# An RWKV-7 recurrence with a feed-forward interleaved: transposes of y, a decay, third blocks and feed-forward pieces change places

## The chip, the cores and the metric

The kernel runs on one core of one Trainium2 chip. The metric is device time in microseconds, the median of several runs. A core has five engines with an instruction queue each: TensorE (PE; the loading of weights is shown apart as PEld), VectorE (DVE), ScalarE (ACT), GpSimd (POOL) and SyncE (SP), which here does nothing but issue DMAs. An engine takes its instructions in program order, so an instruction that waits holds up all that stand behind it on that engine.

## The reference

Two stages. The first is a recurrence over 768 time steps for 4 batches of 8 heads with head size 40; the second sends its output, as 3072 tokens of 320 features, through a feed-forward with 2048 hidden units.

```python
for t in range(S):
    y[:, :, t] = np.einsum('bhd,bhde->bhe', rt, state)
    Sa = np.einsum('bhde,bhe->bhd', state, at)
    state_decay = state * wt[:, :, None, :] - np.einsum('bhd,bhe->bhde', Sa, bt)
    state = state_decay + np.einsum('bhd,bhe->bhde', vt, kt)
...
h = x @ w_in                        # x: (3072, 320)
g = h * np.clip(h + 3.0, 0.0, 6.0) / 6.0
out = g @ w_out
```

## The kernel before

The recurrence is computed in chunks of 64 time steps. A **unit** is one chunk of two of the four batches, all heads: 128 tokens. There are 24 units, numbered 0 to 23; even units hold the state of one pair of batches, odd units that of the other. Within a chunk the steps are solved with a triangular inverse per head, which is made for four units at once: `invert` is a chain of over sixty small DVE operations (L822 and L828), and two **third blocks** per four units (`third_block`, for the first and the last two units) complete the inverse with matmuls in two halves: L858, copies by ACT (L866), then L882, copies by ACT (L892).

The work of a unit is cut into named stages, and a stage into its PE matmuls and what DVE, ACT or POOL make of their result. Ahead of a unit's own turn come W and gam (decay products), A, B, K, factor, F, KB, E and EV. In its turn come RT and VT (transposes of r and v), S (the state transposed, L970), R, C, U, UT, rS, H, and `ysn` (L1099), which gives y and the state's update at once. DVE adds y's parts (L1106) and POOL scales the result into the tile `yg` (L1107). `scale` multiplies the state by the unit's decay: POOL makes the factor (L932, L933), DVE multiplies (L934).

`move` and `move2` bring `yg` into the layout that the feed-forward reads: eight DMAs from `yg` to `xt` on SP's queue (L1147 and L1152), four each. SP also issues all loads of inputs (L470 and L473; the loads for V, B and K of later units are recorded in stages C and KB, in slot 3) and the writes of the output (L1268). They go in the order in which they are recorded.

The feed-forward is a generator that gives a **piece** of PE work at each call. A unit has two jobs; a job has four pieces that expand (`expand`, L1203, each matmul shown as two records, so eight records a piece) and four that contract (`contract`, L1244, four records a piece). Eight short matmuls over the last 64 features (the narrow part) are put in by themselves, mostly at the head of a slot. ACT and DVE (L1218, L1219) form the activation between expansion and contraction, and a job's contraction follows the expansion of the next job. Expansion of a unit can be recorded only when its `move2` has been recorded; on the chip its first matmul waits until the first four DMAs have landed.

The order of all this is written out by hand. Units 0 to 3 have an order of their own. Units 4 to 7 go through `earlier_blocks`: four blocks a unit, each with two halves (`together`), and behind each half as many pieces as `rate / 2` has added up to. From unit 8 on, `slot(i, j)` records the five slots of unit `i` by the list `SLOTS`, where `(5, "W")` is a stage of the unit five later and `(-1, "ysn")` one of the unit before. So y of unit `i - 1` is made in slot 3 of unit `i`. Behind each slot stands a gap:

```python
    def gap(rate, between=None):
        pieces_due[0] += rate
        n = int(pieces_due[0])
        pieces_due[0] -= n
        for k in range(n):
            if between and k == n // 2:
                between()
            piece()
```

`rate` is 3.6 (`DENSE`) while an inversion runs, else 2.7 (`NORMAL`), and 2.2 in units 8 and 9. `between` records half of a third block: for the first two units of each four, in the gaps behind slots 2 and 3. After the last slot, the pieces that are left follow in a row: the tail.

PSUM is taken in pairs of banks; from unit 8 on there are two pairs in turn, which attention stages and third blocks share.

Of the kernel before, what the change touches and what calls it, by code (L numbers as in the profile page):

```python
# [31 lines left out]
def kernel(  # L32
# [47 lines left out]
    NU = 2 * NP  # L80
# [193 lines left out]
    for i, (x, y) in enumerate([(0, DFF // 2), (0, NJ // 2)]):  # L274
        for n, z in enumerate((x, y)):
# [4 lines left out]
            name = ("WA", "BK")[i][n]  # L280
# [164 lines left out]
    NK = NG * NU  # L445
# [101 lines left out]
    def begun_beside():  # L547

        for n, name in enumerate("KB"):
            x = area[:, SCAN + 1 + n * H * JOIN:SCAN + 1 + (n + 1) * H * JOIN]  # L550
            nc.gpsimd.memset(x, 0.0)
            beside[name] = x.rearrange("p (h t) -> p h t", h=H)

    def begun_fixed():

        beside["S"] = grp.tile([P, 2, 2, P], F32, name="S", tag="S", bufs=1)
        nc.gpsimd.memset(beside["S"][:], 0.0)
        beside["E"] = grp.tile([P, H, BL], F32, name="E", tag="U", bufs=1)
        nc.gpsimd.memset(beside["E"][:], 0.0)
# [338 lines left out]
    def third_blocks(first=False):  # L898

        zs = inv.tile([P, 2, 2, H, L], F32, name="zs", tag="x", bufs=1)  # L900
        return [third_block(*third[-1], 2 * n, zs[:, n], first) for n in range(2)]
# [373 lines left out]
    side = deque()  # L1275
    owed, due = [0.0], [0.0]

    def pieces(n):

        owed[0] += n * (8 / 9 if spread[0] else 1)  # L1280
        while owed[0] >= 1:
            owed[0] -= 1
            place[0] = next(stream)
            if not place[0]:
                owed[0] = 0.0

    def aside(n, weight=0):

        for _ in range(n):
            if side and next(side[0], side) is side:  # L1290
                side.popleft()
            due[0] += weight
            while due[0] >= 1:
                due[0] -= 1
                next(weights, None)

    def deal(n):

        for _ in range(n):
            next(weights, None)  # L1300

    def run(stage, steps=0, mixed=0, deals=0):

        for at in stage:
            if at == DONE:
                return
            aside(steps, mixed)
            deal(deals)
# [60 lines left out]
    blocks = {}  # L1369
# [6 lines left out]
    n, cleared = 0, []  # L1376
# [19 lines left out]
    def block(i, j):  # L1396

        if i % NU < 2:
            if j == 0:
                if i % NU == 0:  # L1400
                    blocks[i], blocks[i + 1] = third_blocks()
            run(blocks[i])
# [110 lines left out]
    coming, ahead, own = deque(range(2 * NU, NK)), {}, {}  # L1513

    def a_block(m):

        if coming and begins[coming[0]] == m:
            u = coming.popleft()
            close = coming and begins[coming[0]] < m + BLOCKS
            ahead[u, m] = prepared(u), CLOSE_STAGES if close else AHEAD_STAGES  # L1520
        if m % BLOCKS == 0 and m // BLOCKS + NU < NK:
            i = m // BLOCKS + NU
            own[i, m] = step(i), OWN_STAGES
        parts = {}, {}
        for (u, begin), (fs, order) in sorted(own.items()) + sorted(ahead.items()):
            if m - begin < len(order):
                for name in order[m - begin]:
                    parts[begin % BLOCKS > 0].setdefault(name, []).append(fs[name])
        for k, part in enumerate(parts):
            together(part)  # L1530
            if any(u % NU == NU - 1 and m - begin == 2 and k == (begin % BLOCKS > 0)
                   for u, begin in ahead):
                third.clear()
                side.append(invert(group_F[-1], third))
            yield

    def feed(n, inversion):

        whole = int(n)
        for k in range(whole):  # L1540
            pieces(1)
            aside(inversion)
        pieces(n - whole)

    def earlier_blocks():

        m = 0
        for i in range(NU, 2 * NU):
            spread[0] = i >= 2 * NU - 1
            for j in range(BLOCKS):  # L1550
                rate, inversion = 3.5, 0
                if i < 2 * NU - 1:
                    rate = 2.8
                parts = a_block(m)
                next(parts)
                if side or i % NU == NU - 1:
                    rate, inversion = 6.2, 2 + (i < 2 * NU)
                feed(rate / 2, inversion)
                for _ in parts:
                    pass  # L1560
                if i % NU < 2 and j < 2:
                    if i % NU == 0:
                        aside(3 * L)
                    block(i, j)
                if side:
                    rate, inversion = 6.2, 2 + (i < 2 * NU)
                feed(rate / 2, inversion)
                m += 1

    earlier_blocks()  # L1570


# [4 lines left out]
        [(4, "EV"), (0, "R"), (-1, "H")],  # L1577
        [(5, "A B K factor")],
        [(-1, "ysn"), (0, "C"), (5, "F KB")],
        [(-1, "move move2"), (0, "U UT"), (5, "E"), (0, "rS"), (1, "scale")],  # L1580
    ]
    FIRST_SLOTS = [
        SLOTS[0],
# [8 lines left out]
    NORMAL, DENSE, STEPS_OF = 2.7, 3.6, 2.2  # L1592
    TURNS_NEXT, LEFT = (1, 4), {"e1": 5, "e2": 4, "e3": 3, "e4": 2, True: 1}
    steps_due, pieces_due = [0.0], [0.0]
    units, comings = {u: fs for (u, _), (fs, _) in own.items()}, {u: fs for (u, _), (fs, _) in ahead.items()}

    def piece():

        place[0] = next(stream)
        if side:  # L1600
            steps_due[0] += STEPS_OF
            aside(int(steps_due[0]))
            steps_due[0] -= int(steps_due[0])
        return place[0] is not None

    def gap(rate, between=None):

        pieces_due[0] += rate
        n = int(pieces_due[0])
        pieces_due[0] -= n  # L1610
        for k in range(n):
            if between and k == n // 2:
                between()
            piece()

    def slot(i, j):

        afresh()
        begun, taken = [], {}
        if narrow and (j not in TURNS_NEXT or LEFT[place[0]] < pieces_due[0] + NORMAL):  # L1620
            narrow[0]()
        for k, names_ in (FIRST_SLOTS if i == 2 * NU else SLOTS)[j]:
            u = i + k
            if u >= NK:
                continue
            for name in names_.split():
                if k == 5 and u < 2 * NU + AHEAD:
                    continue
                if name == "W":
                    comings[u] = prepared(u)  # L1630
                if name == "scale":
                    units[u] = step(u)
                rest = (comings if k > 0 and name != "scale" else units)[u][name]()
                fill = [n for n, x in enumerate(FILLS) if name in x]
                if fill:
                    shared[:] = taken.setdefault(fill[0], [None, 0])
                    next(rest)
                    taken[fill[0]][:] = shared
                begun.append((name, rest))
                if name == "F" and u % NU == NU - 1:  # L1640
                    begun.append(("invert", iter(())))
        begun.sort(key=lambda x: AFTER.index(x[0]) if x[0] in AFTER else len(AFTER))
        for _, rest in begun:
            for _ in rest:
                pass
        afresh()
        if begun and begun[-1][0] == "invert":
            third.clear()
            side.append(invert(group_F[(i + 5) // NU], third))

    begun_homes()
    begun_fixed()
    units[2 * NU] = step(2 * NU)
    for _ in units[2 * NU]["scale"]():
        pass
    pairs.clear()
    pairs.append(("pair", 2))
    for i in range(2 * NU, NK + 1):
        for j in range(5):
            if i % NU == 0 and j == 2 and i < NK:  # L1660
                aside(3 * L)
                blocks[i], blocks[i + 1] = third_blocks()
            slot(i, j)
            if i == 2 * NU and j == 1:
                begun_beside()
            gap(DENSE if side else NORMAL if i > 2 * NU + 1 else 2.2,
                (lambda: run(blocks[i])) if i < NK and i % NU < 2 and j in (2, 3) else None)
    spread[0] = False
    while jobs or next(stream):
        next(stream)  # L1670
# [30 lines left out]
```

## Time and profile before

| | |
|---|---|
| median of 3 runs | 820.15 us (818.6 to 824.12) |
| profiled execution | 817.8 us |
| its span, first to last instruction | 816.1 us |
| mean granted TensorE clock | 0.958 |
| DVE, ACT, POOL busy | 487.4, 318.2, 172.3 us |
| feed-forward matmuls, L1203 and L1244 | 254.9 and 230.8 us of PE busy time |
| small DVE steps of the inversion, L822 and L828 | 128.0 us in 360 instructions |

A line of the groups names line, engine, operation, output and inputs, shapes and count; behind the bar stand the busy time, the mean length of one in ns, the idle time of the engine just before and what ended it. In a list of waits a line says who waited for whom, the total in us, how often, and the longest. In a table of windows a line has the stretch and its length, then the busy time and the number of instructions of PE, PEld, DVE, ACT and POOL, the granted clock, the share of the DMA engines and GB/s. In a timeline a line has start, length, engine, line and operation, and in square brackets the idle time before it and what ended it. "issue" stands where the engine waited for nothing that the profile shows.

### The profile page before, as it was taken

The page shows a single profiled execution, that of the slowest core. Times are in us where ns is not written, and L with a number is a line of the kernel's source. Part 1 is how long each engine was busy: PE and PEld are TensorE (multiplying, and loading weights), DVE is VectorE, ACT ScalarE, POOL GpSimd, SP SyncE. Part 2 cuts the span into 40 slices and gives each one's busy share as a digit, 9 for nine tenths or more (in the row PEclk, how much of TensorE's full clock was granted, in tenths as well). Part 3 has the DMA queues.
Part 4 walks back from the last instruction along what each step waited for, and adds up shares of the span by engine and source line. Part 5 has one row for each costly group of instructions (what it writes and reads, how often), then busy time and mean ns, then how long its engine had stood idle before and what let it go on. Part 6 is the DMA issues. An engine that isn't in the chain of part 4 may idle for free.

```text
span 816.1 us, 33536 instructions
## 1 busy us (share of the span) xinstructions
PE 728.8 (89%) x14960; PEld 614.8 (75%) x14960; DVE 487.4 (60%) x967; ACT 318.2 (39%) x646; POOL 172.3 (21%) x322
## 2 busy tenths in 40 slices
PE   5626769999999998999998889998999999999998
PEld 4626658878778787777776778886888888888886
DVE  8897887699545797334886335797436783232210
ACT  2348982313444333542243443334453234321121
POOL 6403003322222304211221221321213021110000
PEclk9855889999999999999999999999999999999999
DMA  9683553311232303221221213222231111100000
GB/s 121 113 194 101 141 135 72 71 28 32 53 70 51 66 19 55 53 45 35 56 48 35 44 33 63 53 45 45 48 56 25 31 27 26 25 19 20 19 9 17
DMA packets 174208, 44.92 MB, mean 55 GB/s; under 512 B 157424, under 2 KB 172784, under 8 KB 174064
## 3 DMA queue, kind: packets, MB, share of 16 engines
q1 hardware_dynamic: 169760, 42.03, 26.2%
q8 instruction: 118, 1.93, 1.0%
q10 hardware_dynamic: 4304, 0.74, 0.6%
q14 instruction: 26, 0.21, 0.1%
HBM read 34.08 MB, written 3.93 MB: 47 GB/s over the span
## 4 chain that ended last, share of the span: by engine, by line
PE 62%; DVE 16%; issue 7%; SPq 5%; ACT 4%; DMA 3%; POOL 1%; ACTq 0%; POOLq 0%; DVEq 0%
PE h L1203 23%; PE o L1244 11%; PE one L1244 7%; DVE prod L822 4%; DVE x L828 4%; PE pair L539 3%; PE pair L1099 3%; SPq L473 3%; PE pair L499 2%; DVE gt L1219 2%; SPq L470 1%; DVE area L565 1%; PE pair L771 1%; PE pair L947 1%; PE pair L997 1%
## 5 line engine op out<-in xcount | busy, mean ns | idle before, releaser
L1203 PE MATMUL h<-xt,win 128*128 128x128 f32 (+1 forms) x2304 | 254.9, 286 | 10.4 <-DMA xt<-yg 7.4
L1203 PEld LDWEIGHTS h<-xt,win 128*128 128x128 f32 (+1 forms) x2304 | 234.2, 195 | 28.3 <-issue 10.5
L1244 PE MATMUL o<-wout,gt 128*128 128x320 f32 x480 | 145.7, 444 | 0.0
L1219 DVE SCALAR_TENSOR_TENSOR gt<-gt,h 128x512 f32<-128x512 f32 x96 | 63.3, 684 | 137.8 <-ACT gt L1218 137.8
L1218 ACT ACTIVATE gt<-h,three 128x512 f32<-128x512 f32 x96 | 62.9, 685 | 167.1 <-PE h L1203 166.9
L1244 PEld LDWEIGHTS o<-wout,gt 128*128 128x128 f32 x480 | 85.9, 190 | 30.9
L1244 PE MATMUL one<-wout,gt 128*128 128x320 f32 x288 | 85.1, 442 | 0.0
L822 DVE TENSOR_TENSOR prod<-x 128x30 f32<-128x30 f32 (+9 forms) x180 | 64.8, 360 | 8.4 <-POOL x L807 3.4
L1244 PEld LDWEIGHTS one<-wout,gt 128*128 128x128 f32 x288 | 52.3, 190 | 19.4
L828 DVE TENSOR_TENSOR x<-x,prod 128x30 f32<-128x30 f32 (+9 forms) x180 | 63.2, 351 | 5.5
L565 DVE COPY_PREDICATED area<-mask,pair 128x512 f32<-128x512 int32 x60 | 44.5, 746 | 32.3 <-PE pair L539 14.7
L1107 POOL TENSOR_TENSOR yg<-ys,gam 128x512 f32<-128x512 f32 x14 | 17.8, 1271 | 191.6 <-DVE ys L1106 144.3
L604 DVE TENSOR_TENSOR_SCAN prods<-area,start 128x528 f32<-128x528 f32 x24 | 30.1, 1259 | 27.1 <-ACT area L584 17.0
L776 ACT ACTIVATE EV<-pair 64x320 f32<-64x320 f32 x44 | 19.0, 431 | 50.9 <-PE pair L947 30.8
L636 POOL COPY gam<-prods 128x256 f32<-128x256 f32 x22 | 12.4, 563 | 108.4 <-DVE prods L604 108.3
L743 POOL TENSOR_TENSOR KBt<-K,rgt 128x320 f32<-128x320 f32 x22 | 19.1, 869 | 60.5 <-ACT rgt L722 58.8
L615 DVE TENSOR_TENSOR_SCAN area<-area,start 128x528 f32<-128x528 f32 x24 | 31.2, 1300 | 0.8
L1106 DVE TENSOR_TENSOR ys<-pair,ys 128x512 f32<-128x512 f32 x16 | 11.1, 691 | 27.9 <-PE pair L1099 27.9
L1099 PEld LDWEIGHTS pair<-area,KBt 64*64 64x64 f32 x1024 | 23.6, 133 | 5.4 <-issue 4.1
L1099 PE MATMUL pair<-area,KBt 64*64 64x104 f32 x1024 | 27.2, 252 | 0.3
L694 ACT ACTIVATE F<-pair 32x256 f32<-32x256 f32 x32 | 11.9, 373 | 34.1 <-PE pair L687 33.9
L637 POOL COPY rgam<-prods 128x256 f32<-128x256 f32 x22 | 24.5, 1114 | 0.0
(300 smaller groups left out, 1101.2 us busy)
## 6 DMA issues: line engine op xcount, KB each, us to landing
V<-in_v_dram SPq DMA_DIRECT2D x96, 40.0 KB
out_dram<-ob SPq DMA_DIRECT2D x47, 80.0 KB
R<-in_r_dram SPq DMA_DIRECT2D x92, 40.0 KB
B<-in_b_dram SPq DMA_DIRECT2D x42, 80.0 KB
K<-in_k_dram SPq DMA_DIRECT2D x42, 80.0 KB
W<-in_w_dram SPq DMA_DIRECT2D x37, 80.0 KB
A<-in_a_dram SPq DMA_DIRECT2D x37, 80.0 KB
xt<-yg SPq DMA_DIRECT2D x72, 40.0 KB
```

Of the source, the lines that this page charges most:

```text
L473: engine.dma_start(out=t[rows, :, 0:D], in_=y.rearrange("h t e -> t h e"))
L565: nc.vector.copy_predicated(out=x[:].rearrange("p (i h) t -> p i h t", i=2), mask=mask8, data=o[2])
L604: nc.vector.tensor_tensor_scan(out=prods[:].rearrange("p r m i -> p (r m i)"), data0=wm[:, 0:SCAN], data1=start[:], initial=0.0, op0=ALU.m ...
L615: nc.vector.tensor_tensor_scan(out=back, data0=back, data1=start[:], initial=0.0, op0=ALU.mult, op1=ALU.add)
L637: nc.gpsimd.tensor_copy(rv[:, :, 0:HB], o["prods"][:, :, 0, 0:HB][:, :, ::-1])
L822: nc.vector.tensor_tensor(out=pv, in0=_ap(x[:], (i + 1) * L + i, [[L, n], [0, i]]), in1=_ap(x[:], i * L, [[0, n], [1, i]]), op=ALU.mult,)
L828: nc.vector.tensor_tensor(out=rest, in0=rest, in1=pv, op=ALU.add)
L1099: nc.tensor.matmul(out=o2[q][half(s), pr, :], lhsT=o[name][half(q), h * D:h * D + SLOT], rhs=beside[name][half(q), 4 * rs + 2 * (s ^ (q * ...
L1203: nc.tensor.matmul(out=hp[c][:, i, :], lhsT=lhsT, rhs=rhs, start=(begun[c] == 0), stop=(begun[c] == 3 * NQ - 1))
L1218: nc.scalar.activation(out=gt[:], in_=hp[c][:], func=AF.Relu, bias=three[:], scale=1.0)
L1219: nc.vector.scalar_tensor_tensor(out=gt[:], in0=gt[:], scalar=6.0, in1=hp[c][:], op0=ALU.min, op1=ALU.mult)
L1244: nc.tensor.matmul(out=op[:], lhsT=gts[c][:, n, :], rhs=wout[:, c * HJ + r * NQ + n, :], start=((split or r == 0) and c == 0 and n == 0), ...
```

## The change

Four things move; no instruction is added or taken away, and the arithmetic is the same.

- In `earlier_blocks` the rate of the blocks of units 4 to 6 is 2.2 instead of 2.8 pieces, so that feed-forward pieces come later. The rate of the gaps of units 8 and 9 is 2.1 instead of 2.2.
- The decay of unit 8, which stood between the last block and the first slot behind two memsets, is recorded behind the third block of unit 7.
- `move` and `move2` of unit `i - 1` are recorded behind the second piece of the gap after slot 3 of unit `i`, not in slot 4. (For unit 7 they stay in slot 2 of unit 8.)
- Third blocks go into other gaps. The first one's halves come behind the third piece after slot 2 and the first piece after slot 3 of the first unit of four; the second one's behind the first piece after slots 0 and 1 of the third unit of four, instead of slots 2 and 3 of the second. These four gaps have the rate 3.6.

```diff
@@ earlier_blocks
                 if i < 2 * NU - 1:
-                    rate = 2.8
+                    rate = 2.2
...
+                if i == 2 * NU - 1 and j == 2:
+                    begun_units[2 * NU] = step(2 * NU)
+                    for _ in begun_units[2 * NU]["scale"]():
+                        pass
@@ SLOTS
-        [(-1, "move move2"), (0, "U UT"), (5, "E"), (0, "rS"), (1, "scale")],
+        [(0, "U UT"), (5, "E"), (0, "rS"), (1, "scale")],
@@
+    THIRDS = {(0, 2): 3, (0, 3): 1, (2, 0): 1, (2, 1): 1}
+
+    def moves(u):
+        for name in ("move", "move2"):
+            for _ in units[u][name]():
+                pass
+
-    def gap(rate, between=None):
+    def gap(rate, between):
...
-            if between and k == n // 2:
-                between()
+            if k in between:
+                between.pop(k)()
             piece()
+        for k in sorted(between):
+            between[k]()
@@ behind begun_fixed()
-    units[2 * NU] = step(2 * NU)
-    for _ in units[2 * NU]["scale"]():
-        pass
@@ the loop over slots
-            gap(DENSE if side else NORMAL if i > 2 * NU + 1 else 2.2,
-                (lambda: run(blocks[i])) if i < NK and i % NU < 2 and j in (2, 3) else None)
+            turn_now = i < NK and (i % NU, j) in THIRDS
+            rate = DENSE if side or turn_now else NORMAL if i > 2 * NU + 1 else 2.1
+            between = {}
+            if j == 3 and 2 * NU < i:
+                between[2] = lambda: moves(i - 1)
+            if turn_now:
+                between[THIRDS[i % NU, j]] = lambda: run(blocks[i - i % NU + i % NU // 2])
+            gap(rate, between)
```

More of the change, by code (lines that the diff above doesn't have):

```diff
@@ L1543, in feed @@
         pieces(n - whole)
+    begun_units = {}
     def earlier_blocks():
@@ L1594 @@
     steps_due, pieces_due = [0.0], [0.0]
-    units, comings = {u: fs for (u, _), (fs, _) in own.items()}, {u: fs for (u, _), (fs, _) in ahead.items()}
+    units, comings = {**begun_units, **{u: fs for (u, _), (fs, _) in own.items()}}, {u: fs for (u, _), (fs, _) in ahead.items()}
     def piece():
```

## The prediction

> **What bounds the kernel.** I read the page's busy rows first, then the stage table, then PE's waits in it.
>
> ```profile
> span 816.1 us, 33536 instructions
> PE 728.8 (89%) x14960; PEld 614.8 (75%) x14960; DVE 487.4 (60%) x967; ACT 318.2 (39%) x646; POOL 172.3 (21%) x322
> ```
>
> PE is busy for 89%. The windows are the blocks of units 4 to 6, of unit 7, the slots of unit 8, units 9 to 24, and the tail:
>
> ```profile
> 195.30:271.00 75.70, 72.56 (x1894) 60.05 (x1893) 41.20 (x74) 37.59 (x88) 19.83 (x36) 1.00 0.32 58
> 271.00:310.40 39.40, 36.39 (x680) 30.72 (x679) 36.65 (x87) 11.63 (x25) 9.50 (x17) 1.00 0.20 37
> 310.40:338.90 28.50, 24.36 (x601) 20.61 (x600) 12.35 (x20) 13.74 (x28) 10.94 (x18) 0.94 0.30 56
> 338.90:772.00 433.10, 412.68 (x8482) 347.65 (x8482) 235.12 (x467) 155.26 (x322) 81.10 (x140) 0.99 0.20 39
> 772.00:816.10 44.10, 40.22 (x266) 32.61 (x264) 5.14 (x8) 6.37 (x11) 0.00 (x0) 1.00 0.06 15
> ```
>
> Length and PE's time are the first two numbers: PE idles 3.1, 3.0, 4.1 and 20.4 us in the four stages before the tail. Work that moves between places where PE is full costs the same in both. So I price the idle, from PE's waits between 195 and 772 us:
>
> ```profile
> PE h L1203 <- DMA xt<-yg: 7.4, 3, 3.6
> PE pair L1055 <- issue: 4.7, 4, 1.6
> PE pair L858 <- DVE bt L660: 4.4, 4, 1.4
> PE pair L970 <- DVE state L934: 2.8, 1, 2.8
> PE pair L882 <- issue: 1.9, 3, 0.8
> PE h L1203 <- DVE start L613: 1.5, 1, 1.5
> ```
>
> Feed-forward waits for its transposed input (L1203), third blocks for a PSUM pair (L858), the ninth unit's S for its decay (L970); L1055 and L882 stand still in the middle of a run for nothing that is shown. A standstill can cost more than its length:
>
> ```profile
> 315.11 0.44 PE L970 MATMUL pair<-ident,state 40*128 40x40 f32 x8 [2.84 <-DVE state L934]
> 315.48 3.67 PE L1203 MATMUL h<-xt,win 128*128 128x128 f32 x16
> ```
>
> and, as windows, the stretch behind it and behind two waits of L1203:
>
> ```profile
> 315.10:319.07 3.97, 3.96 (x24) 3.80 (x24) 2.57 (x3) 1.79 (x4) 1.32 (x2) 0.57 0.33 63
> 369.95:373.00 3.05, 3.05 (x52) 2.83 (x56) 1.55 (x4) 0.00 (x0) 1.47 (x2) 0.52 0.11 30
> 555.00:558.50 3.50, 3.50 (x113) 3.31 (x113) 3.17 (x13) 0.35 (x1) 1.05 (x2) 1.00 0.14 30
> ```
>
> After 2.84 us the granted clock is 0.57 (third number from the right) and sixteen matmuls take 3.67 us, where the chain of waits has 1.98 for sixteen: about 1.6 us more. After 1.89 us (at 369.95) it is 0.52, after 1.85 us (554.99) still 1.00. So I add 1.6 us to a standstill of 1.9 us or more.
>
> **Part 1, feed-forward later.** A piece is 0.99 us of PE if it expands (1.98 for two) and 1.17 if it contracts (2.35 for two). The accumulators give 28 pieces in the blocks of units 4 to 6 instead of 34, 263 instead of 248 in the slots and nine less in the tail. Six pieces, 6.5 us, leave the blocks and return in the slots, nine go from the tail to the slots: zero as long as PE is full. The cover is thinner in the blocks: 1.2 pieces behind each half block instead of 1.4. Ten half blocks have a single piece behind them already, and only one of the halves that follow begins late (0.5 us). I take **+1.5**. Bounds: -3.1 (all idle of this stage goes) and +6.5 (the blocks get no shorter).
>
> **Part 2, the decay.** POOL's scale (0.20 us) and copy and DVE's multiply (0.49 us) go from behind the inversion's copies and two memsets on POOL (311.1 to 314.3) into unit 7's third block. There POOL has been idle for 27 us before 308.3, the state that is scaled was last written at 264.6, and no other unit touches it. DVE gets 0.5 us more while it is busy for 36.65 of 39.40 us, and that delays the transposes at its end, which the third block at 325.7 needs late. Gone: 2.84 us and 1.6 us of half clock, 4.4. Next late is slot 1: ACT evicts RT and VT only until 314.5 us and S behind them, so its products wait for a pair, about 1 us. I take **-3.5**; bounds -4.4 and 0.
>
> [...]
>
> **Part 3, the moves.** In program order they now stand two pieces behind slot 3's products instead of at slot 4. But they are DMAs on SP's queue, behind V, B and K, which slot 3 issues:
>
> ```profile
> 420.24 3.52 SPq L470 DMA_DIRECT2D V<-in_v_dram  x4
> 423.87 1.29 SPq L473 DMA_DIRECT2D B<-in_b_dram  x2
> 425.25 1.28 SPq L473 DMA_DIRECT2D K<-in_k_dram  x2
> 426.58 3.13 SPq L1147 DMA_DIRECT2D xt<-yg  x4
> ```
>
> yg was ready at 418.1, the moves went at 426.6, and PE was released 1.3 us after the fourth. The change passes no more than one output write (1.2 us of SP). So the data come 17 to 18 us after slot 3 begins, as before, and cost or gain is decided by when PE gets there. From unit 14's slots, which have no waits: attention 1.1, 1.6, 1.1, 2.5 and 2.0 us in slots 0 to 4, the narrow matmuls 0.9, half a third block 0.8. For unit 10 of the kernel before: slot 3, 0.9 + 2.5 + three expansions 2.97 = 6.4; slot 4, 2.0 + three contractions and a fourth that ends it 4.7 = 6.7; slot 0, 1.1: 14.2 us, against 17.85 until the data are there, so 3.65 late; the trace has 3.62. With the pieces of the changed kernel:
> - unit 10: 17.4 against 19.1 (an output write now goes first): 1.7 late
> - unit 11: 16.0 against 17.5: 1.5 late
> - unit 12: 18.7 against 18.5: not late
> - unit 13: 17.4 against 18.0: 0.6 late
> - unit 14: 15.2, and 1.1 that its slot 3 lost to DVE, against 18.0: 1.7 late
> - unit 15: 13.9 against 17.3: 3.4 late
> - unit 16: 14.9 against 16.5: 1.6 late
>
> The seven sum to 10.5. Units 8 and 9 have two more gaps and come after their data; from unit 17 on SP has no inputs left to fetch and the data come in time. A mid-run standstill that stays in unit 11's way makes it 9.5, and unit 15 costs 1.6 of clock: 11.1. Before: 1.89 + 1.52 + 3.62 + 1.85 = 8.9 (the wait put down to L613 ends 1.36 after the moves, so it is one of them), and two clock drops: 12.1. I take **-1.0**. Bounds: -12.1 (nothing is late), +18 (all six 2 us later and slowed).
>
> **Part 4, third blocks.** First halves at slot 2 waited 1.37, 1.15, 1.15 and 0.73 us (the 4.4 of L858). The first block now goes behind three pieces, over 3 us, so slot 2's evictions are done; but it then stands right before slot 3, whose second pair waits for its four ACT copies (1.5 us), beside ysn's 1.6: about 0.3 four times. The second block goes behind one piece after slot 0, where RT and VT are evicted 1.9 us after the slot begins and PE arrives after 2.1 to 2.3. 0.1 each where a relu (0.69) stands first. Sum **-2.8**; bounds -4.4 and +4.4 (L858's wait at all eight places).
>
> **Part 5, mid-run standstills.** 4.7 + 1.9 = 6.6 us in seven places, all in slots 3 and 4 behind a third block and gaps of two or three pieces. Units 9 and 13 lose their block there (0.60 + 0.85 + 0.76 = 2.2 us). At the other four gaps have up to one piece more; half of 4.4. **-4.4**; bounds -6.6 and +2 (they come up behind slot 0).
>
> [...]
>
> **Sum:** 1.5 - 3.5 - 1.0 - 2.8 - 4.4 = -10.2. The profiled execution took 817.8 us (its span is 816.1), so 807.6; the median of the runs is 820.15, so **810.0**.
>
> **Rivals.**
> - *Late data (slower).* The second place in this sum that can turn: if units 10, 11 and 13 to 16 reach their data 2 us earlier than worked out (PE fuller of pieces, SP kept up), they idle 10.5 + 12 = 22.5 us and five drop the clock, 8: 30.5 instead of 12.1. Then +18.4 for -1.0: **829**. For it: the kernel before ran into just this four times, and nine pieces more bring feed-forward nearer to its data. Against: the working gives 3.65 for 3.62.
> - *Waits come back.* DVE or ACT, not PE, sets slots 8 to 16, and each wait that goes appears one slot on; the decay and the thinner blocks alone remain, -2: **818**. For it: DVE is 93% busy in unit 7. Against: 54% in units 9 to 24.
> - *The moves do land earlier*, by the two to three pieces that they stand earlier: the lateness goes, -10 more: **800**. Against: SP's order above.
>
> **Chances.** Forecast 0.55 (own range 803 to 816), late data 0.13, waits come back 0.22, earlier moves 0.10. The range 799 to 821 leaves out the slower rival and little else. 1% is 8.2 us, about what a measurement of this kernel can tell from none: under 812 lies most of the forecast and the earlier moves, 0.53; 0.34 within; 0.13 slower.
>
> **What would show it.** L970's wait gone and the clock 1.00 near 315 us; the blocks up to unit 7 ending some 5 us sooner; a tail of about 34 us; waits of L1203 for xt near units 14 to 16 in place of those at 370, 400 and 431 us; L858 near zero; the four issues of xt still right behind V, B and K. I am wrong if xt waits exceed 15 us, or if units 4 to 6 stay at 75 us.

## The result

| | before | after |
|---|---|---|
| median | 819.69 us (20 runs) | 814.96 us (20 runs) |
| ratio | | 0.994, interval 0.9917 to 0.9963 |
| profiled execution, span | 817.8, 816.1 us | 815.24, 813.6 us |
| stretches at half clock between 195 us and TensorE's last matmul | 3 x 3.41 us | 4 x 3.41 us |

The changed kernel is 0.6% faster, 4.7 us. Forecast were 10.2 us: the sign is right and the size about half. The interval lies wholly below 1, but the gain is smaller than 1%, which the prediction took for about the least that a measurement of this kernel can show. The head of the page of the changed kernel:

```profile
span 813.6 us, 33528 instructions
PE 728.0 (89%) x14960; PEld 614.5 (76%) x14960; DVE 487.8 (60%) x967; ACT 318.1 (39%) x646; POOL 170.9 (21%) x322
```

The same five stages of the changed kernel as windows (length, then busy time and number of instructions of PE, PEld, DVE, ACT, POOL; then granted clock, DMA share, GB/s):

```profile
196.60:270.60 74.00, 66.80 (x1858) 55.17 (x1857) 40.49 (x72) 36.40 (x86) 19.95 (x36) 1.00 0.31 57
270.60:308.80 38.20, 35.27 (x667) 29.53 (x665) 35.12 (x88) 11.39 (x25) 8.45 (x19) 1.00 0.24 44
308.80:336.20 27.40, 25.24 (x618) 20.71 (x618) 14.37 (x21) 14.62 (x30) 10.97 (x17) 1.00 0.30 57
336.20:779.70 443.50, 428.49 (x8587) 362.48 (x8587) 236.44 (x469) 157.32 (x325) 81.48 (x140) 0.98 0.19 38
779.70:813.60 33.90, 29.98 (x192) 23.84 (x190) 3.85 (x6) 4.67 (x8) 0.00 (x0) 0.97 0.07 19
```

Length minus PE's time is what PE idles: 7.2, 2.9, 2.2, 15.0 and 3.9 us, where before had 3.1, 3.0, 4.1, 20.4 and 3.9. From the first window to the end 620.8 us became 617.0, that is 3.8 less: 3.4 of idle and 0.4 of PE's busy time. (The stretch ahead of the first window was 1.3 us longer. Its length differs by up to 4.5 us between executions of kernels that are the same there, so I compare from the first window on.) PE's waits in the changed kernel between 195 and 772 us (total, times, longest):

```profile
PE h L1203 <- DMA xt<-yg: 8.3, 3, 3.9
PE h L1203 <- DVE area L615: 2.7, 1, 2.7
PE pair L858 <- ACT EV L776: 2.3, 1, 2.3
PE pair L947 <- DVE area L565: 2.1, 1, 2.1
PE pair L771 <- ACT VT L958: 1.4, 1, 1.4
PE pair L687 <- ACT ys L1061: 1.2, 1, 1.2
PE pair L687 <- issue: 1.0, 2, 0.7
PE pair L1099 <- DVE bt L660: 0.9, 2, 0.7
...
PE pair L499 <- DVE ys L1132: 0.8, 1, 0.8
...
PE pair L1055 <- issue: 0.7, 1, 0.7
```

L970's wait is gone, so are L858's four and nearly all standstills of L1055 and L882. What grew is the wait for xt: the line put down to L615 ends 1.2 us after the fourth DMA of its unit and is one of them, so they sum to 11.4 us with one of 0.4 that stands further down, against 8.9. One such place, on SyncE and on TensorE: the wait for unit 15's y, which PE reaches in the first slot of unit 17.

```profile
568.63 3.12 SPq L470 DMA_DIRECT2D V<-in_v_dram  x4
571.86 1.97 SPq L473 DMA_DIRECT2D B<-in_b_dram  x2
573.92 1.28 SPq L473 DMA_DIRECT2D K<-in_k_dram  x2
575.26 3.12 SPq L1147 DMA_DIRECT2D xt<-yg  x4
```

```profile
575.38 0.39 PE L970 MATMUL pair<-ident,state 40*128 40x40 f32 x8
579.67 5.51 PE L1203 MATMUL h<-xt,win 128*128 128x128 f32 x38 [3.90 <-DMA xt<-yg]
```

yg was complete at 566.7 us. The DMAs that transpose it went 8.5 us later, behind the loads, and PE stood for 3.90 us.

### The profile page after: what moved, and what is told of

The parts are those of the page before. It is cut to its first block, busy times and chain, and to the rows that moved or that the text cites. A ratio compares the mean times of both kernels' runs of the same rounds, so it can differ in the third digit from the quotient of the medians.

```text
span 813.6 us, 33528 instructions
## 1 busy us (share of the span) xinstructions
PE 728.0 (89%) x14960; PEld 614.5 (76%) x14960; DVE 487.8 (60%) x967; ACT 318.1 (39%) x646; POOL 170.9 (21%) x322
## 3 DMA queue, kind: packets, MB, share of 16 engines
q8 instruction: 118, 1.93, 1.0%
## 4 chain that ended last, share of the span: by engine, by line
PE 62%; DVE 21%; ACT 5%; issue 4%; SPq 3%; DMA 2%; POOL 1%; DVEq 0%; ACTq 0%
PE h L1203 22%; PE o L1244 10%; PE one L1244 8%; DVE prod L822 4%; DVE x L828 4%; PE pair L539 3%; PE pair L1099 3%; DVE area L615 2%; DVE prods L604 2%; PE pair L499 2%; DVE gt L1219 2%; SPq L473 1%; PE pair L1039 1%; PE pair L1055 1%; PE pair L997 1%
## 5 line engine op out<-in xcount | busy, mean ns | idle before, releaser
L1203 PE MATMUL h<-xt,win 128*128 128x128 f32 (+1 forms) x2304 | 256.5, 287 | 13.0 <-DMA xt<-yg 8.3
L1203 PEld LDWEIGHTS h<-xt,win 128*128 128x128 f32 (+1 forms) x2304 | 235.9, 195 | 31.5 <-issue 14.2
L1244 PE MATMUL o<-wout,gt 128*128 128x320 f32 x480 | 146.0, 444 | 0.0
L1244 PEld LDWEIGHTS o<-wout,gt 128*128 128x128 f32 x480 | 85.7, 190 | 31.3 <-issue 0.4
L1244 PE MATMUL one<-wout,gt 128*128 128x320 f32 x288 | 85.3, 441 | 0.3 <-issue 0.3
L1244 PEld LDWEIGHTS one<-wout,gt 128*128 128x128 f32 x288 | 52.1, 190 | 19.4 <-issue 0.4
L615 DVE TENSOR_TENSOR_SCAN area<-area,start 128x528 f32<-128x528 f32 x24 | 31.0, 1290 | 0.8
L1099 PEld LDWEIGHTS pair<-area,KBt 64*64 64x64 f32 x1024 | 23.4, 132 | 5.5 <-issue 3.9
L1099 PE MATMUL pair<-area,KBt 64*64 64x104 f32 x1024 | 26.6, 251 | 1.0 <-DVE bt L660 0.9
L722 ACT ACTIVATE rgt<-pair 128x320 f32<-128x320 f32 x16 | 7.0, 438 | 41.4 <-DVE kt L757 37.1
```

What stands on the lines that cost most here:

```text
L615: nc.vector.tensor_tensor_scan(out=back, data0=back, data1=start[:], initial=0.0, op0=ALU.mult, op1=ALU.add)
L1099: nc.tensor.matmul(out=o2[q][half(s), pr, :], lhsT=o[name][half(q), h * D:h * D + SLOT], rhs=beside[name][half(q), 4 * rs + 2 * (s ^ (q * ...
L1203: nc.tensor.matmul(out=hp[c][:, i, :], lhsT=lhsT, rhs=rhs, start=(begun[c] == 0), stop=(begun[c] == 3 * NQ - 1))
L1244: nc.tensor.matmul(out=op[:], lhsT=gts[c][:, n, :], rhs=wout[:, c * HJ + r * NQ + n, :], start=((split or r == 0) and c == 0 and n == 0), ...
```

## The experiments

Each run is compared with the kernel before, run on the same chip. All compute the whole result. Stage lengths are those of the profiled executions.

### Each part alone

**The decay alone**: before, with the decay of unit 8 in unit 7.

```diff
+                if i == 2 * NU - 1 and j == 2:
+                    begun_units[2 * NU] = step(2 * NU)
...
-    units[2 * NU] = step(2 * NU)
```

> The kernel before with only unit 8's decay moved. Theory A (the sum of the prediction, part 2): the wait of L970 (2.84 us) and the half clock behind it (1.6 us) go, about 1 us comes back in slot 1 as waits for pairs; the waits for xt in units 8 to 14 stay as they are, since they hang on the distance from slot 3 to the expansion alone. 816 us against 819.7 (-3.5). Rival B: PE is only earlier at the next wait (xt of unit 8 at 370 us), which grows by what the decay saved: 819 to 820.

Measured: 822.25 against 823.58 us, 0.9986 (0.9956 to 1.0015). Unit 8 takes 24.0 us instead of 28.5, L970's wait is gone, and units 9 to 16 take 244.5 instead of 242.1. Its waits of PE between 195 and 772 us:

```profile
PE h L1203 <- DMA xt<-yg: 5.3, 3, 3.3
PE pair L858 <- DVE bt L660: 4.4, 4, 1.4
PE pair L1055 <- issue: 3.9, 3, 1.9
PE h L1203 <- DVE prod L822: 3.3, 1, 3.3
...
PE h L1203 <- DVE start L613: 1.8, 1, 1.8
```

The three lines of L1203 are waits for xt and sum to 10.4 us, 1.5 more than before, so more than half of the 2.4 us that units 9 to 16 lose is lateness. The saving is real where it is made, and part of it is lost again; the interval holds both none of it and 3.6 us.

**The later feed-forward alone**: before, with the rate of the early blocks at 2.2.

```diff
-                    rate = 2.8
+                    rate = 2.2
```

> The kernel before with only the rate of the blocks of units 4 to 6 at 2.2 instead of 2.8, so every later piece comes some seven pieces later. Theory A (data arrival decides): by the slot costs of the prediction the expansions of units 8 to 16 begin 23 to 34 us behind slot 3, the data need 17 to 19, so all four waits for xt (8.9 us) and the three drops of the clock behind them go, -12 us; the blocks of units 4 to 6 get only about 1.7 us shorter for 6.5 us fewer pieces (as in the trace of the changed kernel), +5: 812 to 813. Rival B (moving pieces is free, the gain of the change is in its other three parts): 819 to 821, or slower by the thinner cover alone, 825.

Measured: 807.3 us, 0.9823 (0.9791 to 0.9854). This single number brings three times what the whole change brings. Its stages and its waits between 195 and 772 us:

```profile
196.10:270.20 74.10, 66.63 (x1859) 54.99 (x1857) 40.47 (x72) 36.45 (x86) 20.11 (x36) 1.00 0.32 57
...
339.70:753.50 413.80, 407.28 (x8473) 344.49 (x8473) 232.46 (x465) 154.92 (x320) 81.63 (x140) 1.00 0.21 40
753.50:805.00 51.50, 47.66 (x314) 38.50 (x313) 6.43 (x10) 7.64 (x13) 0.00 (x0) 1.00 0.06 15
```

```profile
PE pair L858 <- DVE bt L660: 4.5, 4, 1.4
PE pair L970 <- DVE state L934: 3.8, 1, 3.8
PE pair L858 <- ACT EV L776: 2.3, 1, 2.3
```

No wait of L1203 for xt is left. The data of units 8 to 16 are first expanded 22 to 34 us after the products that give y (`ysn`, in slot 3), when they have long landed, because six pieces more are still to be done ahead of them; in the kernel before, the units that waited came to theirs after 17 to 19 us, the wait included. Units 9 to 24 take 413.8 us instead of 433.1, although the thin early blocks cost what they cost in the whole change (74.1 us, with the same new wait of L858 for EV) and the tail is 7.4 us longer. The gain, 14.6 us by the ratio, is twice the 7 us of the first theory, and lateness is not all of it. PE idles 6.5 us in units 9 to 24 instead of 20.4: 8.9 of the difference are the waits for xt, and 5.4 are standstills of L1055 and L882, which are gone as well, although the third blocks stand where they stood (one of 0.5 us at L997 came for them). With both edits, later feed-forward and decay:

> The kernel before with the rate of 2.2 in the blocks of units 4 to 6 and the decay moved, third blocks and moves as before. Theory A: on top of the later pieces (ratio 0.982) the wait of L970, 3.76 us there, and the half clock behind it go, less about 1 us that comes back in slot 1: ratio 0.977 to 0.978. Rival B (the decay's saving is eaten by the next wait, as it was mostly when it was moved alone): 0.981 to 0.982, and then the loss must stand as a longer wait in units 8 to 16.

Measured: 802.65 us, 0.9775 (0.9734 to 0.9815). L970's 3.8 us are gone, unit 8 takes 26.2 us instead of 31.4. In the medians the decay now brings half a per cent, as the first theory has it; but this interval and that of the later feed-forward alone (0.9791 to 0.9854) overlap, so the size is not settled.

**The third blocks alone**: before, with the new gaps and their rate of 3.6.

```diff
+    THIRDS = {(0, 2): 3, (0, 3): 1, (2, 0): 1, (2, 1): 1}
...
+            rate = DENSE if side or turn_now else NORMAL if i > 2 * NU + 1 else 2.2
```

> The kernel before with only the third blocks in their new gaps and the rate of 3.6 there; the blocks of units 4 to 6 keep 2.8. Theory A (data arrival decides): nothing holds the feed-forward back, so the denser gaps bring it to its data too early: by the slot costs of the prediction the expansions of units 8 to 18 begin 8 to 14 us behind slot 3 where the data need 15 to 19, 62 us of lateness in eleven units instead of 9, with a half clock of 1.6 us behind most of them, less some 5 us of waits of third blocks: 870 to 895. Rival B (the third blocks' new gaps are a gain of their own): 813 to 818.

Measured: 894.82 us, 1.0889 (1.0805 to 1.0972). And the whole change without its later feed-forward (rate 2.8 in the early blocks):

> The changed kernel with the blocks of units 4 to 6 at 2.8 again. Theory A: every expansion comes six to eight pieces earlier, 5 to 10 us behind slot 3 in units 8 to 17, 93 us of lateness instead of 11, and the clock behind most: 895 to 930. Rival B (the later feed-forward only costs, 5 us of thinner cover): 810.

Measured: 902.78 us, 1.0986 (1.0907 to 1.1064). The first line of PE's waits between 195 and 772 us, of the third blocks alone and then of the change at 2.8:

```profile
PE h L1203 <- DMA xt<-yg: 58.0, 15, 8.3
```

```profile
PE h L1203 <- DMA xt<-yg: 80.3, 12, 10.9
```

Four gaps of every twenty with 3.6 instead of 2.7 pieces use the feed-forward up faster than y comes. From then on PE arrives ahead of the data at nearly every unit (15 and 12 such waits). The mean clock of the two profiled executions is 0.916 and 0.907, against 0.958, so the waits cost more than their length. This is the rival "late data" of the prediction, and the later feed-forward is what kept the change out of it.

**The moves alone undone**: the whole change, with the moves in slot 4 again.

```diff
-        [(0, "U UT"), (5, "E"), (0, "rS"), (1, "scale")],
+        [(-1, "move move2"), (0, "U UT"), (5, "E"), (0, "rS"), (1, "scale")],
```

> The changed kernel with the moves recorded in slot 4 again, as before. Theory A: SP issues V, B and K first in either case, so the data land at the same time and the waits for xt stay at about 11 us: 815, within 0.3% of the changed kernel. Rival C (the moves' place is worth two pieces): xt waits grow by 2 us in each of units 10 to 16, 825 or more.

Measured: 815.95 us, 0.9914 (0.9883 to 0.9945); the whole change has 0.994 (0.9917 to 0.9963). The waits for xt are 2.65, 0.71, 0.34, 3.20, 2.06 and 0.25 us, 9.2 in all, where the whole change has 11.4. The new place is worth nothing that can be measured, as SyncE's order says.

### What the data's lateness is worth

**Moves ahead of the loads**: the whole change, with the moves recorded right behind ysn, so ahead of V, B and K on SyncE.

```diff
-        [(-1, "ysn"), (0, "C"), (5, "F KB")],
+        [(-1, "ysn move move2"), (0, "C"), (5, "F KB")],
```

> The changed kernel with the moves recorded directly behind ysn in slot 3, ahead of the loads of V, B and K on SP's queue. Theory A: the moves are issued when yg is ready, about 4.1 us behind the start of slot 3, and the data land some 8.6 us behind it instead of 17 to 18; every expansion from unit 8 on begins 10 us or more behind slot 3, so all waits for xt go (11.4 us) with the drops of the clock behind them (3 to 5 us): 799 to 802. V, B and K come some 3 to 6 us later, needed two slots or more behind: no price. Rival D (PE is the bound there, and what is saved at L1203 comes back at the next stage, or V, B and K are late in their turn): 812 to 815.

Measured: 802.67 us, 0.9757 (0.973 to 0.9785). SyncE for unit 15's y, which was ready at 562.25 us:

```profile
562.27 3.11 SPq L1147 DMA_DIRECT2D xt<-yg  x4
565.43 2.48 SPq L1152 DMA_DIRECT2D xt<-yg  x4
568.01 2.97 SPq L470 DMA_DIRECT2D V<-in_v_dram  x4
```

No wait for xt is left, and none appears for the loads that now go later. So the lateness was the order of one queue. The same edit in the kernel before:

> The kernel before with the moves recorded directly behind ysn in slot 3, ahead of the loads of V, B and K, and nothing else changed. Theory A: data land 8.6 us behind slot 3, the shortest distance of an expansion from unit 8 on is 14 us: the four waits for xt (8.9 us) and the drops of the clock behind them (3.2 us) go, the wait of L970, the third blocks' and the mid-run standstills stay: ratio to the kernel before 0.985. Rival D (only later pieces help, since feed-forward that lies further behind keeps all engines looser): 0.995 to 1.0.

Measured: 810.76 us, 0.987 (0.9826 to 0.9913). Units 9 to 16 take 232.9 us instead of 242.1: the 8.9 us of waits are gone and one of two half-clock stretches with them, while L858 waits 1.9 us longer (6.3 in all). L970's wait and the standstills stay.

### The other parts, with nothing late

In the next three the moves stand ahead of the loads, so that no gain can come back as lateness, and the early rate is the 2.8 of before.

**Decay**, third blocks as before:

> The kernel before with the early rate 2.8 kept and the third blocks where they were, with two edits: the moves are recorded right behind ysn, ahead of the loads of V, B and K on SP, and the decay of the ninth unit is begun two blocks earlier. It asks whether the decay's saving is lost to the waits on xt. Theory A (it is: decay alone gave 4.5 us in unit 8 and 2.6 us of it came back as later waits on xt; with the moves first there is no such wait): the whole 4 us remains on top of the 0.987 of the moves alone, so a ratio of 0.981 to 0.983, some 806 us, with no wait on xt. Theory B (the saving is lost to something else, such as the feed-forward being used up and the standstills): 0.986 to 0.988.

Measured: 808.04 us, 0.9835 (0.9807 to 0.9864). That is just short of the 0.981 to 0.983 of the first theory, and the interval overlaps that of the moves alone. Unit 8 takes 27.0 us. L970's wait is gone, but 1.0 us of L499 and 0.4 of L771 came for it, and the half clock of that stage came back at another place (below).

**Third blocks in the new places, at the normal rate**: the run above, with

```diff
-            rate = DENSE if side or turn_now else NORMAL if i > 2 * NU + 1 else 2.1
+            gap(DENSE if side else NORMAL if i > 2 * NU + 1 else 2.2, between)
```

(shown against the changed kernel's line).

> The kernel above (moves first, decay early, early rate 2.8), with the third blocks at their new places but at the normal rate of the gaps, so without the denser 3.6 of the change. It asks whether the third blocks' new places bring anything, apart from the pieces that the denser rate uses up. Theory A (the places take away the waits of the pair product L858 and part of the unit-8 waits, 2.8 us as predicted, and the density is what cost 8.9% alone): 2 to 4 us below the run with the old places, ratio 0.977 to 0.979, some 801 to 803 us. Theory B (the places bring nothing without the pieces): the same ratio as with the old places.

Measured: 801.24 us, 0.9756 (0.9724 to 0.9787), 6.8 us below the run above on the same chip, more than the 2 to 4 us of the first theory. Its waits between 195 and 772 us:

```profile
PE pair L1055 <- issue: 3.2, 3, 1.3
PE pair L947 <- DVE area L565: 1.6, 1, 1.6
...
PE pair L858 <- DVE bt L660: 0.5, 2, 0.3
```

and its slots of units 9 to 24:

```profile
339.80:755.20 415.40, 408.48 (x8482) 344.44 (x8482) 234.32 (x467) 155.32 (x322) 81.58 (x140) 1.00 0.20 40
```

With the very pieces of before (8482 records), PE idles 6.9 us there. It is 20.4 us in the kernel before and 12.9 in the run above, where the moves already stand ahead of the loads; the third blocks' places bring the last 6.0, and 5.9 of them are L858's (6.4 us to 0.5). The places of the third blocks are good; their density was not. This run and the changed kernel with the moves ahead of the loads have the lowest ratios (0.9756 and 0.9757), well under either kernel; the next run and later feed-forward with the decay lie within their intervals.

**The same with an early rate of 2.5**:

> The same as the one above with the early rate 2.5, about three pieces fewer ahead of the slots. It asks whether there is an early price for fewer pieces once nothing waits for xt. Theory A (no unit waits for xt any more, so fewer pieces early only thin the cover of the early blocks and make the tail longer): the same as at 2.8 within 1.5 us, ratio 0.976 to 0.981. Theory B (later pieces still shorten the middle, by pieces that the late units would otherwise lack): 3 us or more below the run at 2.8, ratio below 0.975.

Measured: 803.19 us, 0.9766 (0.9737 to 0.9794): the same. Once nothing is late, later pieces bring nothing.

### The standstills

**64 transposes more on TensorE, ahead of the first stage**, in the kernel before; nothing reads them.

```diff
+    spare = bank("one", [P, 512], 1)
+    for n in range(64):
+        nc.tensor.transpose(out=spare[:, 0:P], in_=ident[:], identity=ident[:])
```

> The kernel before with 64 transposes that nothing reads, recorded on TensorE ahead of the first stage; nothing else differs. It asks where the standstills come from that the trace puts down to issue in mid-run (eight or so of 0.3 to 1.9 us, at record numbers of TensorE some 127 or 128 apart, each just behind the landing of a 16 KiB packet of the instruction queue). Theory A (TensorE stands at the edge of a block of instructions that has not landed yet): the standstills stay at the same record numbers counted from the start, so each stands 64 records earlier in the program than before, at other products and other lines. Theory B (a dependency of those products that the trace does not show): they stay at the same products of the same units, 64 records later. The time is within 1% of the kernel before under both, since the 64 transposes take 4 to 7 us at the start, beside the loads that TensorE waits for there.

Measured: 820.36 and 834.15 us, against 820.69. The profiled execution is the longer one; it had a clock of 0.927 and six waits for xt, so I read only places from it, no times. All seven standstills of L1055 and L882 are gone from their products, although these and what they depend on are the same. The wait at L771 (1.5 us at matmul record 5220), which is no standstill on the grid below, moved by 64 to 5284, as a dependency does. One new standstill stands at record 6046, some 127 records ahead of 6173, where before has one. The two waits that are put down to issue in this execution, between 201 and 789 us:

```profile
PE pair L771 <- issue: 1.5, 1, 1.5
...
PE pair L687 <- issue: 0.3, 1, 0.3
```

So the second theory falls. The first is right that the edges count, and wrong that each edge keeps its standstill: with other products ahead of them most edges cost nothing (in the kernel before 68 of the 76 below). (The longer waits and the lower clock of this execution, from 319 us on, may have covered some.)

Where the edges lie can be read in the kernel before. One standstill, in the middle of a run of equal products for which the profile shows no wait:

```profile
458.07 0.45 PE L1055 MATMUL pair<-RT,S 40*64 40x64 f32 x14
460.10 0.47 PE L1055 MATMUL pair<-RT,S 40*64 40x64 f32 x17 [1.58 <-issue]
```

and what came in just ahead of it, in the DMA view of the stretch from 457.5 to 458.8 us:

```profile
q8 instruction: 1, 0.02, 4.5%
```

That is a 16 KiB packet on the queue for instructions (all 118 packets of that queue have this size in the kernel before). Its transfer ended at 458.71 us, and the products went on 1.39 us later. The standstills of the kernel before between 195 and 790 us that are put down to issue and last 0.25 us or longer, that of L771 left out, stand at the matmul records 4398, 6173, 6680, 6808, 8456, 8583, 9090 and 10993. Their distances are multiples of some 126.8 records, 52 of them from the first to the last. I laid a grid of 126.8 records, fixed at record 6173, over the kernel before: 76 edges between 228 and 707 us. The eight standstills, of 0.50 to 1.58 us, stand each within two records of an edge, and each ends 1.32 to 1.46 us after a packet landed. At seven of the eight the 127 matmuls ahead had run in 3.8 us or less, at the eighth (record 4398) in 5.0. Of the 53 edges with 5 us or more ahead, that is the only one with a standstill. In the changed kernel the five such waits (records 4398, 7188, 8329, 8584 and 10360, 0.27 to 0.79 us) stand within three records of the same grid and end 1.29 to 1.50 us after a packet landed. That a run of small products uses up its instructions faster than the next packet comes is my reading of these distances and times; no run changed the packets, so it was not shown.

## Why the prediction was half right

By its own steps, in us of the profiled executions. Half clock is put at 1.7 us for each stretch of 3.41 us, an estimate: half of it, as the granted clock was 0.50 there and PE was busy for 3.38 to 3.41 us of each.

| part | forecast | measured | from |
|---|---|---|---|
| 1 feed-forward later | +1.5 | +4.0 | idle of units 4 to 7, 6.1 to 10.1 |
| 2 decay | -3.5 | -2.4 | -2.8 (L970) - 1.7 (clock) + 1.4 (L771) + 0.8 (L499) |
| 3 lateness | -1.0 | +5.9 | waits 8.9 to 11.4; half-clock stretches behind them 2 to 4 |
| 4 third blocks | -2.8 | -3.5 | -4.4 (L858) + 0.9 (L1099) |
| 5 standstills | -4.4 | -4.6 | 6.6 to 2.0 (L687, L1055, L1244) |
| sum | -10.2 | -0.6 | measured in all -3.8 |

Of the 3.2 us between the last two, 1.1 are a wait of L997 that went; 2.1 are PE's busy time, and I can't place them. The median, 814.96 us, lies inside the prediction's own range (803 to 816) but nearer to the 818 of "waits come back" than to 810.0, so the number alone does not speak for its mechanism.

- **Part 1 was mis-sized.** Six pieces left the early blocks, PE's busy time fell by 5.8 us there, and the stage became only 1.7 us shorter. I had counted half blocks that begin late. What came was a third block behind a single piece that waited 2.25 us for the eviction of EV (L858 at 226 us). The bounds held it. That the pieces come back in the slots and in the tail was right (33.9 us against some 34). The sign that it named for being wrong, units 4 to 6 staying at 75 us, nearly came: 74.0.
- **What part 1 left out is larger than what it priced.** I took later pieces as a shift between full places, so zero, and put their effect on the lateness into part 3, for the sequence with all edits at once. That hid that two edits pull against each other: alone, later pieces gain 14.6 us of 823.58 (1.8%) and the third blocks in denser gaps lose 8.9%.
- **Part 2** has the mechanism right, and one successor: L771 behind ACT's eviction of VT (1.4 us). It had not the 0.8 us of L499 behind DVE. Together they cost 2.2 us instead of about 1.
- **Part 3's waits were right, its clock was not.** Forecast were 10.5 us in units 10 to 16, 1.5 of them in unit 11; measured are 2.66, 0, 0, 0.44, 1.93, 3.90 and 2.44, sum 11.4. SyncE's order held, the moves' place is worth nothing, and "the moves land earlier" fell. But I gave the clock 1.6 us, for unit 15 alone, by a length of 1.9 us. It was four half-clock stretches, 6.8 us, behind the waits of 2.66, 1.93 and 3.90 us. This is the step that failed most: -1.0 was forecast for this part, and the rows give +5.9.
- **Part 4** was right in size for its waits (L858). It left out what the denser gaps do by themselves, above. The places are worth 6.8 us when nothing is late; in the profiles that is 6.0 us of idle in units 9 to 24, nearly all L858's, and three half-clock stretches fewer, while the stretch ahead of the first window came out 4.2 us longer.
- **Part 5** was right in size, at least in part by luck. It gave as the reason that third blocks move away and gaps grow. But the later feed-forward alone, which does neither, has lost all seven (one of 0.5 us came at L997); 64 transposes that nothing reads took all seven off their products; and with the third blocks in their new places at the normal rate L1055 and L882 stand still for 4.4 us again. In these runs an edge of the grid of 126.8 records cost something with some products ahead of it and nothing with others: 8 of 76 edges in the kernel before, and none of those at L1055 and L882 once 64 transposes stood ahead.
- "Waits come back" (818) holds for unit 8 and the early blocks, where PE now waits for ACT's evictions (L771, L858). In slots 8 to 16, where the rival stood, it was mostly data and clock that came back, not DVE or ACT (0.9 us of L1099 behind DVE).

## What the runs showed that I had not expected

The clock. My 1.9 us was not a rule: 1.89 us at 369.95 dropped the clock, 1.85 at 554.99 did not, and in the run with the decay and the moves ahead of the loads (third blocks as before) a standstill of 1.24 us did. The half-clock stretches lie on a grid in these two traces. They begin at 315.47, 370.08 and 431.52 us in the kernel before, each 3.413 us long, and lie 16.0 and 18.0 times that length apart; in the changed one they begin at 426.04 (two in a row, 6.827 us), 545.51 and 579.64, 35.0 and 10.0 times apart. Windows cut on that grid, of the kernel before (the clock is the third number from the right):

```profile
366.67:370.08 3.41, 1.52 (x9) 0.84 (x6) 1.84 (x3) 1.76 (x5) 0.59 (x2) 1.00 0.19 53
370.08:373.49 3.41, 3.41 (x72) 3.19 (x75) 1.43 (x4) 0.00 (x0) 1.34 (x2) 0.50 0.15 33
373.49:376.90 3.41, 3.41 (x68) 3.31 (x62) 1.13 (x2) 0.86 (x2) 0.00 (x0) 1.00 0.35 58
...
550.98:554.39 3.41, 2.15 (x8) 1.17 (x7) 3.00 (x6) 2.08 (x6) 0.27 (x1) 1.00 0.23 66
554.39:557.80 3.41, 2.81 (x76) 2.73 (x76) 3.15 (x11) 0.00 (x0) 1.66 (x3) 1.00 0.08 21
```

In the first PE was busy for 1.52 of 3.41 us, and the whole next window was granted half. The wait of 1.85 us fell across an edge, 1.25 and 0.60 us, and cost its length alone. The same wait of 2.25 us at L858, in the changed kernel and then in the one with the moves ahead of the loads:

```profile
224.65:228.06 3.41, 2.08 (x70) 1.68 (x71) 1.58 (x4) 2.11 (x6) 1.52 (x3) 1.00 0.33 64
228.06:231.47 3.41, 3.41 (x84) 2.64 (x82) 1.32 (x3) 0.85 (x2) 0.00 (x0) 1.00 0.13 39
```

```profile
224.33:227.74 3.41, 1.63 (x68) 1.35 (x69) 2.03 (x5) 1.67 (x5) 1.52 (x3) 1.00 0.39 65
227.74:231.15 3.41, 3.41 (x71) 2.65 (x69) 0.00 (x0) 1.29 (x3) 0.00 (x0) 0.50 0.13 43
231.15:234.57 3.42, 3.42 (x16) 2.20 (x14) 1.20 (x3) 0.00 (x0) 0.00 (x0) 0.50 0.08 19
```

One wait, one place in the program: nothing in one execution, two stretches of half clock (3.4 us, by the estimate above) in the other. Up to there the two kernels are the same. What differs is where the grid lies against the program: PE was busy for 2.08 us of the window in which the wait falls in the one, and for 1.63 in the other. The boundary is not a busy time alone: one window of the changed kernel with 1.60 us (fourteen matmuls of the feed-forward) left the clock alone, while in the run with the decay and the moves ahead of the loads one with 2.10 us (119 small ones) dropped it, and one with 2.15 us (118 small ones) in the kernel before did not. I cut the kernel before and the changed one on their grids, from 190 us to TensorE's last matmul. Of the windows at full clock five have less than 1.5 us of matmul time, and half clock followed each of them; six have 1.5 to 2.1 us, and it followed one (the 1.52 above); 342 have more, and it followed none. What decides in between, whether small products count for less, and why half clock lasts one window at some places and two at others, was not tried.

## What to carry to other kernels

Price a reordering by when each consumer reaches its data, and look first at the queue that brings them: recording the transposes of y ahead of eight loads on SyncE gave 1.3% here, moving them in the program while they stayed behind those loads gave nothing that could be measured. A change of several parts can be the sum of a strong gain and a strong loss; one part alone, or all but one, shows it. And a part alone can gain by something else than its reason, as later pieces did by the standstills. In these traces a wait of one to three microseconds had no fixed price: one of 1.85 us cost its length alone, one of 1.89 us was followed by a stretch of 3.41 us at half clock, and one of 2.25 us by none in one execution and by two in another, 1.7 and 3.4 us more by the estimate above. This belongs into the range of a forecast, not into its middle.
